# Attention over a dilated window and a long convolution: a new step order, with PSUM pool and copy engine chosen per step

## The chip, the cores and the metric

The kernel runs on one core of one Trainium2 chip. The metric is device time in microseconds (us) of one execution. The kernel before takes 263.62 us, the median of three runs (262.68 to 266.32).

The engines are TensorE (PE in the profile: matmuls and transposes; PEld: its weight loads), VectorE (DVE), ScalarE (ACT), GpSimd (POOL), and SyncE (SP), which only issues transfers here. Transfers between DRAM and SBUF, and within SBUF, are run by 16 DMA engines. Matmul results land in PSUM and have to be copied out by VectorE or ScalarE before TensorE may use the place again; this copy is called evacuation below.

## The reference

Two independent halves share the program, and their outputs are concatenated along the last axis.

```python
def _A_ref(x, wqkv, wo):                       # S=2048, D=576, 32 heads of 18
    W, dil = 8, 2
    qkv = (x @ wqkv) ...                       # q, k, v
    idx = pos[:, None] - off[None, :]          # 8 positions back, in steps of 2
    logits = einsum("bhsd,bhswd->bhsw", q, kg) * scale    # kg, vg: gathered k, v
    logits = where(idx >= 0, logits, -1e9)
    o = einsum("bhsw,bhswd->bhsd", softmax(logits), vg)
    return o.reshape(B, S, D) @ wo

def _B_ref(q, k, v, shift_k, ssm_k, ssm_D):
    k_shift = ...                              # 4-tap causal convolution of k along S
    kv = k_shift * v
    y = irfft(rfft(kv, 2S) * rfft(ssm_k, 2S))[:S]         # causal convolution, length S
    return q * (y + kv * ssm_D)

out = concatenate([a, b], axis=-1)
```

All tensors are bf16.

## The kernel before

The program is a list of some 300 steps. Each is a short Python function that emits a few instructions; the string `ORDER` says in which order they are emitted. A scheduler below it may still move an instruction a little, as far as data allows. The instruction stream of each engine is then fixed: an engine that waits for something lets nothing behind pass.

Half A: `xt` transposes x by TensorE, `qk` and `qt` project q and k (`qt` for the last 64 channels), `v` projects v, `lm` multiplies q by shifted k on VectorE, `lb` sums over a head's channels by TensorE, `sa`/`sb` are the softmax, `at` transposes the weights, `ha` copies v's edge rows to the neighbouring partition, `pm` multiplies weights by v, `ps` sums over the window by TensorE, `po` is the output projection. Half B: `sk` and `cv` are the short convolution, `ia` makes tables, `sx`/`kp` are the first stage of the transforms of kv and of the filter, whose results go to DRAM (`Dx`, `Dk`), `kl`/`xl` load them in another layout, `ks`/`xs` are the second stage, `gp` is the product of the spectra, `gi` the first stage back (to `Dy` in DRAM), `yl` loads that, `ys` is the last stage, with the multiplication by q. `kt` transposes the filter.

```python
pa = tile_pool(name="pa", bufs=2, space=PS)      # PSUM: two places in each of two pools,
pb = tile_pool(name="pb", bufs=2, space=PS)      # each [128, 2, 512] fp32
def psa(): return pa.tile([128, 2, 512], FP32, name="psA")
def psb(): return pb.tile([128, 2, 512], FP32, name="psB")
...
nc.scalar.dma_start(shr, B_shift_k ...)          # loads ahead of the steps, on SyncE's queue
load_x(0)
load_wq()                                        # q and k columns of wqkv, 1.3 MB
load_x(1)
load_kv(0)
load_x(2)
load_x(3)
...
def x_tr(qtr):                                   # one step: three groups of transposes
    for kp in range(3):
        ptr = pa.tile([128, 2, 1024], BF16, name="psA")
        ...                                      # 8, 8 and 4 transposes
        if kp == 1:
            nc.scalar.activation(dst, ptr[:, 0:n, 0:512], ACT.Copy)      # L288
        else:
            copy32(dst, ptr[:, 0:n, 0:512])      # L275, VectorE, as int32
...
nc.scalar.activation(wqt, wq.rearrange(...)[:, :, :, 128 * HC:D], ACT.Copy)   # L429
...
def qk_step(comp, cp, j):
    ps = psa()
    for u in range(2):
        for kb in range(5):
            nc.tensor.matmul(ps[:, u, :], wcols(kb, comp, 2 * cp + u), xT[:, kb, t], ...)   # L381
    nc.scalar.activation(..., ps[:], ACT.Copy)                                              # L382

def s1_part(src, key, c2, ch, Dd, add_d):        # sx and kp
    ps = psb()
    ...                                          # L417: 2 matmuls of 384 columns
    nc.scalar.activation(vst[:, :, 384 * ch:384 * ch + 384], ps[:, :, 0:384], ACT.Copy)     # L421
    if ch == 2:
        for dh, (d0, d1) in enumerate(DCH):
            nc.sync.dma_start(by_f1(Dd, dh, 4 * c2, 4), ...)     # to Dx or Dk; vst has two slots

def s2(Wt, g, dst, scale):                       # ks and xs: four groups each
    for prl in range(4):
        ps = psb()
        ...                                      # L549: 2 matmuls of 288 columns
        nc.scalar.activation(dst[:, 2 * prl:2 * prl + 2, :], ps[:, :, 0:HD], ACT.Copy, scale=scale)  # L551

def w_load(Dd, key, i):                          # kl, xl; Wr has three slots, shared with yl
    nc.sync.dma_start(Wr.get((key, i)), by_rt(Dd, i // 4, i % 4))

def k_spec(i):                                   # ks; Kr has two slots
    Kc = Kr.get(i)
    s2(Wr[("k", i)], i % 4, Kc[:, 0], 1.0 / 2048)
    nc.gpsimd.dma_start(Kc[0:64, 1], Kc[64:128, 0])      # the swap of the halves, within SBUF
    nc.gpsimd.dma_start(Kc[64:128, 1], Kc[0:64, 0])

def g_inv(i, hv):                                # gi; Yr has two slots
    for prl in (2 * hv, 2 * hv + 1):
        ps = psb()
        ...                                      # L582: 4 matmuls of 288 columns
        nc.scalar.activation(Y[:, 2 * prl:2 * prl + 2, :], ps[:, :, 0:HD], ACT.Copy)   # L584
    if hv:
        nc.sync.dma_start(by_rt(Dy, dh, g), Y)

def y_load(i):                                   # needs all four Dy stores of its half
    nc.sync.dma_start(Wr.get(("y", i)), by_f1(Dy, dh, 8 * c4, 8))
    nc.gpsimd.dma_start(qtr.get(i), qb[...])
# y_step (ys): L657, 4 matmuls; L658, the VectorE product that also empties PSUM
# p_sum (ps): L618; p_mul (pm): L604; p_out (po): L637, L639; l_mul (lm): L486; l_sum (lb): L496, L502
```

Of the kernel before, what the change touches and what calls it, by code (L numbers as in the profile page):

```python
# [9 lines left out]
ACT = mybir.ActivationFunctionType  # L10
# [8 lines left out]
xt.0 sk qk.0.0.0 qk.1.0.0 cv.0 qk.1.1.0 qk.0.1.0 lkv.1 xt.1 xt.2 qk.0.1.1 lkv.2 xt.3 ia qk.1.0.1 sx.0.0 lwv sx.0.1  # L19
qk.1.1.1 sx.0.2 sx.1.0 qk.1.0.3 sx.1.1 cv.1 sx.1.2 qk.0.0.1 sx.2.0 cv.2 sx.2.1 sx.2.2 qk.1.0.2 sx.3.0 lkn qt.0  # L20
qk.1.1.2 sx.3.1 qk.0.0.2 sx.3.2 sx.4.0 qk.0.1.2 sx.4.1 qk.0.0.3 sx.4.2 lkv.3 sx.5.0 qt.3 cv.3 sx.5.1 qk.0.1.3 qt.2
sx.5.2 qt.1 qk.1.1.3 sx.6.0 kt.0 v.1 sx.6.1 v.2 sx.6.2 v.0 sx.7.0 lm.0.0 sx.7.1 kt.1 sx.7.2 kp.0.0 lm.1.0 lm.0.1
lm.0.2 lb.0 lm.1.1 lm.1.2 kp.0.1 lm.2.0 lb.1 v.3 kp.0.2 kp.1.0 v.4 v.5 lm.3.0 ha.0 lm.2.1 kp.1.1 kt.2 kp.1.2 kp.2.0
lm.2.2 lb.2 kp.2.1 lm.3.1 lm.3.2 v.7 lb.3 kt.3 kp.2.2 v.6 lm.4.0 kt.4 kp.3.0 kp.3.1 kp.3.2 kp.4.0 sa.0 kp.4.1 kp.4.2
kt.5 kp.5.0 lm.4.1 sb.0 v.8 lm.4.2 lm.5.0 v.9 lb.4 lm.5.1 v.10 kt.6 kp.5.1 v.11 kp.5.2 lm.5.2 lb.5 kp.6.0 at.0 ha.1
v.13 kt.7 lm.6.0 v.15 lm.6.1 kp.6.1 v.14 ha.2 kp.6.2 kp.7.0 lm.6.2 lb.6 kp.7.1 v.12 lm.7.0 lm.7.1 lwo lm.7.2 ha.3
kp.7.2 kl.0 xl.0 lb.7 ks.0 xs.0 kl.1 xl.1 ks.1 sa.1 kl.2 pm.0.0 ps.0.0 gp.0.0 gi.0.0 pm.0.1 xl.2 xs.1 gp.0.1 pm.1.0
gp.1.0 ps.0.1 ks.2 xl.3 xs.3 gp.1.1 xs.2 gi.0.1 gp.2.0 gi.1.0 xl.4 ps.1.0 gp.2.1 gi.1.1 kl.3 kl.4 gi.2.0 pm.1.1 ks.3
pm.2.0 ps.1.1 po.0.0 xs.4 ks.4 po.0.1 gp.3.0 xl.5 gi.2.1 pm.2.1 kl.5 ps.2.0 gp.3.1 ks.5 po.1.0 sb.1 pm.3.0 ps.2.1
gi.3.0 po.1.1 gp.4.0 gp.4.1 at.1 gi.3.1 kl.6 ps.3.0 pm.3.1 xs.5 pm.4.0 po.2.0 gp.5.0 xl.6 gi.4.0 ps.3.1 gp.5.1 gi.4.1  # L30
yl.0 xs.6 ks.6 ys.0.0 xl.7 gi.5.0 po.2.1 ps.4.0 kl.7 ks.7 pm.4.1 po.3.0 xs.7 gp.6.0 ys.0.1 ps.4.1 gi.5.1 yl.1 gi.6.0
gp.6.1 gp.7.0 po.3.1 pm.5.0 yl.2 ys.1.0 po.4.0 pm.5.1 ys.1.1 gi.6.1 ys.2.0 pm.6.0 ps.5.0 gi.7.0 ps.5.1 gp.7.1 gi.7.1
yl.3 po.4.1 pm.6.1 ys.2.1 yl.4 ps.6.0 ys.3.0 ys.3.1 po.5.0 po.5.1 pm.7.0 yl.5 ps.6.1 ys.4.0 ys.4.1 po.6.0 ys.5.0 yl.6
ps.7.0 po.6.1 yl.7 ys.5.1 pm.7.1 ps.7.1 ys.6.0 ys.6.1 po.7.0 ys.7.0 ys.7.1 po.7.1
# [4 lines left out]
def kernel(  # L39
# [19 lines left out]
    HC = 4  # L59
# [16 lines left out]

    def psa():
        return pa.tile([128, 2, 512], FP32, name="psA")

    def psb():  # L80
        return pb.tile([128, 2, 512], FP32, name="psB")
# [146 lines left out]
    def load_wq():  # L228
        nc.sync.dma_start(wq[:, 0:4, :], A_wqkv[0:512, 0:2 * D].rearrange("(kb p) a -> p kb a", p=128))
        nc.sync.dma_start(wq[0:64, 4, :], A_wqkv[512:576, 0:2 * D])  # L230
# [25 lines left out]
    load_x(0)  # L256
    load_wq()
    load_x(1)
    load_kv(0)
    load_x(2)  # L260
    load_x(3)

# [11 lines left out]
    def copy32(dst, src):  # L274
        nc.vector.tensor_single_scalar(dst.bitcast(I32), src.bitcast(I32), 0, ALU.bitwise_or)  # L275

    def x_tr(qtr):
        for kp in range(3):
            n = 2 if kp < 2 else 1
            ptr = pa.tile([128, 2, 1024], BF16, name="psA")  # L280
            for u in range(n):
                kb = 2 * kp + u
                col0 = 128 * kb
                for lsb in range(4):
                    nc.tensor.transpose(ptr[:, u, 128 * lsb:128 * lsb + 128], xns[qtr][:, lsb, col0:col0 + 128], ident[:])
            dst = xT[:, 2 * kp:2 * kp + n, 512 * qtr:512 * qtr + 512]
            if kp == 1:
                nc.scalar.activation(dst, ptr[:, 0:n, 0:512], ACT.Copy)  # L288
            else:
                copy32(dst, ptr[:, 0:n, 0:512])  # L290
# [73 lines left out]
    def v_step(t2):  # L364
        ps = psa()
        for di, (d0, d1) in enumerate(DCH):
            for kb in range(5):
                nc.tensor.matmul(ps[:, di, 0:288], xTt[:, kb, t2, :], wv[:, kb, d0:d1], start=(kb == 0), stop=(kb == 4))  # L368
        nc.scalar.activation(vX[:, 14 + t2, :].rearrange("p (d i h) -> p d i h", i=2, h=16),
                             ps[:, :, 0:288].rearrange("p i (h d) -> p d i h", d=DH), ACT.Copy)  # L370
# [4 lines left out]
    def qk_step(comp, cp, j):  # L375
        pad = PADL if comp else 0
        ps = psa()
        t = slice(512 * j, 512 * j + 512)
        for u in range(2):
            for kb in range(5):  # L380
                nc.tensor.matmul(ps[:, u, :], wcols(kb, comp, 2 * cp + u), xT[:, kb, t], start=(kb == 0), stop=(kb == 4))  # L381
        nc.scalar.activation((k2 if comp else q2)[cp][:, :, pad + 512 * j:pad + 512 * j + 512], ps[:], ACT.Copy)  # L382

    def qk_tail_step(j):
        ps = psa()
        hh, t = j // 2, slice(512 * j, 512 * j + 512)
        for kb in range(5):
            nc.tensor.matmul(ps[:, 0, :], wqt[:, kb].rearrange("p c d -> p (c d)"), xT[:, kb, t], start=(kb == 0), stop=(kb == 4))
        r, o = slice(64 * hh, 64 * hh + 64), 512 * (j % 2)
        nc.scalar.activation(qh[r, o:o + 512], ps[0:64, 0, :], ACT.Copy)  # L390
        nc.scalar.activation(kh[r, PADL + o:PADL + o + 512], ps[64:128, 0, :], ACT.Copy)
        if j == 1:
            nc.scalar.activation(kh[64:128, 0:PADL], ps[64:128, 0, 512 - PADL:512], ACT.Copy)

    def ia_tables():
        for g in range(8):
            ps = psb()
            for v in range(4):
                for zi in range(2):
                    for hp in range(2):  # L400
                        nc.tensor.matmul(ps[64 * hp:64 * hp + 64, zi, 128 * v:128 * v + 128],
                                         W2[:, 4 * g + v, zi].rearrange("p l f -> p (l f)"),
                                         nident[:] if hp > zi else ident[:], start=True, stop=True, tile_position=(0, 64 * hp))
            nc.scalar.activation(IAt[:, :, 4 * g:4 * g + 4, :].rearrange("p z v t -> p z (v t)"), ps[:], ACT.Copy)
        ptr = pb.tile([128, 2, 1024], BF16, name="psB")
        for ri in range(2):
            nc.tensor.transpose(ptr[:, 0, 128 * ri:128 * ri + 128], T1[:, ri, :], ident[:])
        nc.vector.tensor_copy(IB[:], ptr[:, 0, 0:256].rearrange("p (a b) -> p a b", a=2))


    def s1_part(src, key, c2, ch, Dd, add_d):
# [9 lines left out]
        nc.scalar.activation(vst[:, :, 384 * ch:384 * ch + 384], ps[:, :, 0:384], ACT.Copy)  # L421
# [7 lines left out]
    nc.scalar.activation(wqt, wq.rearrange("p k (c d) -> p k c d", c=2)[:, :, :, 128 * HC:D], ACT.Copy)  # L429

    def sk_step():
        for i in range(3):
            n = 256 if i < 2 else 64
            ps = psb()
            for u in range(2 if i < 2 else 1):
# [3 lines left out]
            nc.scalar.activation(skb[:, :, 256 * i:256 * i + n],  # L439
                                 ps[:].rearrange("p u (d j) -> p j (u d)", j=4)[:, :, 0:n], ACT.Copy)  # L440
# [19 lines left out]
    def k_tr(c2):  # L460
        kt = ktr.get(c2)
        ptr = pb.tile([128, 2, 1024], BF16, name="psB")
# [28 lines left out]
    def l_sum(n):  # L491
# [13 lines left out]
        nc.scalar.activation(Lh[hf][:, 2 * wp:2 * wp + 2, :], psw[:, 0, :].rearrange("p (u t) -> p u t", u=2), ACT.Copy)  # L505
# [28 lines left out]
    def at_step(hf):  # L534
        L = Lh[hf].rearrange("p w (a b) -> p w b a", b=2)
        pst = pa.tile([128, 2, 4, 2, 128], BF16, name="psA")
# [4 lines left out]
        for u in range(2):  # L541
            nc.scalar.activation(ath[hf][:, 4 * u:4 * u + 4].rearrange("p w b j h -> p w b (j h)"), pst[:, u], ACT.Copy)  # L542


    def s2(Wt, g, dst, scale):
        for prl in range(4):
# [4 lines left out]
            nc.scalar.activation(dst[:, 2 * prl:2 * prl + 2, :], ps[:, :, 0:HD], ACT.Copy, scale=scale)  # L551
# [11 lines left out]
    def x_spec(i):  # L563
        s2(Wr[("x", i)], i % 4, Xr.get(i), 1.0)
        Wr.drop(("x", i))
# [8 lines left out]
    def g_inv(i, hv):  # L574
        dh, g = i // 4, i % 4
        Y = Yr[i] if hv else Yr.get(i)
        for prl in (2 * hv, 2 * hv + 1):
# [6 lines left out]
            nc.scalar.activation(Y[:, 2 * prl:2 * prl + 2, :], ps[:, :, 0:HD], ACT.Copy)  # L584
# [26 lines left out]
    def p_sum(tp, u):  # L611
        if u == 0:
            oTr.get(tp)
            oaccs[tp] = pa.tile([128, 2, 4, 128], FP32, name="psA")
# [8 lines left out]
        nc.scalar.activation(oTr[tp][:, 0:4].rearrange("p c u t -> p u c t"), oaccs[tp][:], ACT.Copy)  # L623
# [4 lines left out]
        nc.scalar.activation(oTr[tp][:, 4, 0, :], otl[:, 0, 0:128], ACT.Copy)  # L628
        tlr.drop(tp)

    def p_out(tp, u):
# [7 lines left out]
        nc.scalar.activation(stage[:, u, :].rearrange("p (i d) -> p i d", i=2), ps[:, :, 0:288], ACT.Copy)  # L639
# [25 lines left out]
    STEP = dict(xt=x_tr, ia=ia_tables, sk=sk_step, qk=qk_step, qt=qk_tail_step, lkv=load_kv, lwv=load_wv, lkn=load_knat,  # L665
# [3 lines left out]
    for item in ORDER.split():  # L669
        name, *args = item.split(".")  # L670
        STEP[name](*map(int, args))

# [29 lines left out]
```

## Time and profile before

| Engine | what most of its time is | busy, us | mean of one, ns |
|---|---|---|---|
| TensorE | L381, q and k projections, 160 matmuls | 40.7 | 403 |
| TensorE | L618, window sums, 512 matmuls | 40.2 | 227 |
| ScalarE | L551, evacuations of ks and xs, 64 | 38.0 | 652 |
| ScalarE | L421, evacuations of sx and kp, 48 | 37.4 | 811 |
| VectorE | L486, q times shifted k, 32 | 37.9 | 1225 |
| VectorE | L604, weights times v, 16 | 36.6 | 2289 |

The profiled execution spans 265.8 us, and its DMA queues move 55.24 MB, 208 GB/s on average. A page of the profile gives the busy time of each engine, then the span in 40 equal slices (one digit for each slice and engine: tenths busy; PEclk is the granted clock of TensorE in tenths), the chain of work that ended last, followed back from the end, and the costliest groups of instructions by line of the kernel. A busy TensorE isn't TensorE at its peak, since matmuls overlap; and idle time of an engine matters only where the chain runs through it.

### The profile page before, as it was taken

Reading aid. Unit: us, or ns where it says so; the run is one execution under the profiler, and the core shown is the slowest. Engines: PE = TensorE matmul, PEld = TensorE weight load, DVE = VectorE, ACT = ScalarE, POOL = GpSimd, SP = SyncE. Lnnn points to the kernel's source line nnn. Section 1 sums busy time; section 2 is a strip of 40 time slices with the busy share of each in tenths; the row PEclk is TensorE's granted clock in tenths of the full one; section 3 lists DMA queues with packets and bytes.
Section 4 is the critical chain, followed back from the end, with each engine's and each line's share of the span. In section 5 each row is a group of like instructions: output and inputs, shape, how many; then the busy total and the mean of one; then the engine's idle time right before and its main releaser. Section 6 shows DMA issues by size and latency. Waiting matters only on the chain.

```text
span 265.8 us, 4987 instructions
## 1 busy us (share of the span) xinstructions
PE 228.5 (86%) x2013; PEld 153.0 (58%) x2013; DVE 190.5 (72%) x211; ACT 173.2 (65%) x252; POOL 25.2 (9%) x62
## 2 busy tenths in 40 slices
PE   2689899999999999996946799796999881999893
PEld 2225665444573747565614676575987660698782
DVE  1667989999968878989647798847496484277232
ACT  0566978978984657968466699694789761162321
POOL 8700000000000000002010110030200210101100
PEclk9999999999999999999995999998999998599999
DMA  7999943823433435737799869389678899157994
GB/s 239 307 333 370 304 109 113 249 71 111 126 91 120 132 92 149 209 86 202 240 231 316 274 166 306 154 252 302 168 260 270 239 230 313 35 165 228 325 293 133
DMA packets 43759, 55.24 MB, mean 208 GB/s; under 512 B 2285, under 2 KB 36285, under 8 KB 43737
## 3 DMA queue, kind: packets, MB, share of 16 engines
q1 hardware_dynamic: 41766, 47.71, 59.4%
q0 software_dynamic: 1968, 7.23, 10.1%
q8 instruction: 15, 0.25, 0.4%
q14 instruction: 8, 0.06, 0.1%
q10 hardware_dynamic: 2, 0.00, 0.0%
HBM read 29.27 MB, written 18.87 MB: 181 GB/s over the span
## 4 chain that ended last, share of the span: by engine, by line
PE 57%; DMA 24%; ACT 12%; issue 2%; SPq 2%; DVE 1%; POOL 0%; ACTq 0%; DVEq 0%; POOLq 0%
PE psA L381 13%; DMA area<-area 7%; DMA area<-Dy 7%; PE psA L368 7%; PE psA L618 7%; PE psB L417 5%; PE psA L502 5%; PE psA L637 5%; PE psB L549 4%; PE psB L657 3%; DMA area<-in_A_wqkv_dram 3%; PE psB L582 3%; ACT area L421 2%; DMA area<-Dk 2%; DMA Dy<-area 2%
## 5 line engine op out<-in xcount | busy, mean ns | idle before, releaser
L604 DVE TENSOR_TENSOR area<-area,area 128x4096 bf16<-128x4096 bf16 x16 | 36.6, 2289 | 7.7 <-PE psA L618 3.2
L551 ACT ACTIVATE area<-psB 128x576 bf16<-128x576 f32 x64 | 38.0, 652 | 6.2 <-PE psB L549 3.3
L421 ACT ACTIVATE area<-psB 128x768 bf16<-128x768 f32 x48 | 37.4, 811 | 7.1 <-PE psB L417 6.7
L381 PE MATMUL psA<-area,area 128*128 128x512 bf16 x160 | 40.7, 403 | 1.3 <-ACT area L288 1.3
L486 DVE TENSOR_TENSOR area<-area 128x2048 bf16<-128x2048 bf16 x32 | 37.9, 1225 | 4.7 <-PE psA L502 4.7
L618 PE MATMUL psA<-ident,area 128*128 128x128 bf16 x512 | 40.2, 227 | 0.2 <-ACT area L623 0.2
L618 PEld LDWEIGHTS <-area 128*128 128x128 bf16 x512 | 35.2, 102 | 4.4 <-DVE area L604 0.6
L549 PE MATMUL psB<-area,W 128*128 128x288 bf16 x128 | 27.0, 301 | 10.8 <-DMA area<-Dx 4.8
L568 DVE TENSOR_TENSOR area<-area,area 128x2304 bf16<-128x2304 bf16 x16 | 21.2, 1355 | 16.2 <-DMA area<-area 15.0
L381 PEld LDWEIGHTS <-area 128*128 128x128 bf16 x160 | 16.0, 102 | 22.5 <-issue 7.5
L658 DVE TENSOR_TENSOR area<-psB,area 128x576 bf16<-128x576 f32 x16 | 11.7, 754 | 20.3 <-PE psB L657 18.6
L584 ACT ACTIVATE area<-psB 128x576 bf16<-128x576 f32 x32 | 19.9, 656 | 9.8 <-PE psB L582 7.0
L637 PE MATMUL psA<-wv,area 128*128 128x288 bf16 x160 | 26.2, 296 | 0.1
L639 ACT ACTIVATE area<-psA 128x576 bf16<-128x576 f32 x16 | 10.4, 652 | 23.8 <-PE psA L637 19.6
L417 PE MATMUL psB<-area,T 128*128 128x384 bf16 x96 | 22.2, 327 | 1.8 <-ACT area L421 1.6
L368 PE MATMUL psA<-wv,area 128*128 128x288 bf16 x160 | 23.0, 288 | 0.7 <-ACT area L542 0.7
L446 DVE TENSOR_TENSOR area<-area,area 128x2304 bf16<-128x2304 bf16 x16 | 21.5, 1353 | 2.4 <-ACT area L439 2.2
L368 PEld LDWEIGHTS <-area 128*128 128x128 bf16 x160 | 20.0, 145 | 5.0 <-issue 4.1
L382 ACT ACTIVATE area<-psA 128x1024 bf16<-128x1024 f32 x16 | 16.4, 1023 | 9.8 <-PE psA L381 9.7
L549 PEld LDWEIGHTS <-W 128*128 128x128 bf16 x128 | 12.2, 101 | 18.0 <-issue 8.0
L582 PE MATMUL psB<-area,IAt 128*128 128x288 bf16 x128 | 19.9, 290 | 3.1 <-DVE area L568 1.8
L648 POOL DMA_DIRECT2D area<-in_B_q_dram x8 | 6.1, 766 | 147.0 <-PE psA L540 116.0
(116 smaller groups left out, 295.6 us busy)
## 6 DMA issues: line engine op xcount, KB each, us to landing
Dx<-area SPq DMA_DIRECT2D x16, 288.0 KB, 3.1
Dk<-area SPq DMA_DIRECT2D x16, 288.0 KB, 3.4
area<-Dk SPq DMA_DIRECT2D x8, 576.0 KB, 6.3
area<-Dx SPq DMA_DIRECT2D x8, 576.0 KB, 5.2
area<-area POOLq DMA_DIRECT2D x16, 288.0 KB, 6.6
Dy<-area SPq DMA_DIRECT2D x8, 576.0 KB, 5.0
out_dram<-area SPq DMA_DIRECT2D x16, 288.0 KB, 3.7
area<-Dy SPq DMA_DIRECT2D x8, 576.0 KB, 7.9
```

Of the source, the lines that this page charges most:

```text
L368: nc.tensor.matmul(ps[:, di, 0:288], xTt[:, kb, t2, :], wv[:, kb, d0:d1], start=(kb == 0), stop=(kb == 4))
L381: nc.tensor.matmul(ps[:, u, :], wcols(kb, comp, 2 * cp + u), xT[:, kb, t], start=(kb == 0), stop=(kb == 4))
L417: nc.tensor.matmul(ps[:, ri, 0:384], T1[:, ri, :], sf[:, 384 * ch:384 * ch + 384], start=True, stop=not extra)
L421: nc.scalar.activation(vst[:, :, 384 * ch:384 * ch + 384], ps[:, :, 0:384], ACT.Copy)
L446: nc.vector.tensor_tensor(dst, kfull[:, 4 * c + 3 - j:4 * c + 7 - j, :], skb[:, j, :].unsqueeze(1).to_broadcast([128, 4, D]), ALU.mult)
L486: nc.vector.tensor_tensor(dst[:, u], halves(q2[h], hf), halves(k2[h][:, :, shs[u]:shs[u] + S], hf), ALU.mult)
L549: nc.tensor.matmul(ps[:, hp, 0:HD], W2[:, 8 * g + 2 * prl + hp].rearrange("p i l f -> p (i l f)"), Wt[:, 2 * prl + hp, :], start=True, sto ...
L551: nc.scalar.activation(dst[:, 2 * prl:2 * prl + 2, :], ps[:, :, 0:HD], ACT.Copy, scale=scale)
L582: nc.tensor.matmul(ps[:, hp, 0:HD], IAt[:, zi, 8 * g + hl, :], Pp[(i, hv)][:, zi, hl % 4, :], start=(zi == 0), stop=(zi == 1))
L604: nc.vector.tensor_tensor(P.rearrange("p w (d h) -> p w d h", h=H), vs[:, :, 0:16], at.to_broadcast([128, W, 16, H]), ALU.mult)
L618: nc.tensor.matmul(oaccs[tp][:, u, ct, :], P[:, wi, 128 * ct:128 * ct + 128], ident[:], start=(ct == 0 and wi == 0), stop=(wi == W - 1 and ...
L637: nc.tensor.matmul(ps[:, di, 0:288], lhs, wot[:, ct if ct < 4 else 4 + u, d0:d1], start=(ct == 0), stop=(ct == 4))
```

## The change

It leaves every operation of the computation as it is and touches three things. The first is the order of the steps, with the loads of x, of wq (now in two halves, q's columns and k's) and of the short filter's inputs placed among them, and the copy `wqt` as a step of its own. The second is a suffix on a step: `a` or `b` names the PSUM pool, `v` or `s` the engine that evacuates (VectorE or ScalarE); without a suffix it stays at the default. The third is that a transposition of x becomes three steps, one for each pair of channel blocks, which may go apart. Order, pools and engines come from a model of the engines' queues. The aim is that TensorE waits less for free PSUM places, for copies behind others in one queue, and for transfers.

```diff
 ORDER = """
-xt.0 sk qk.0.0.0 qk.1.0.0 cv.0 qk.1.1.0 qk.0.1.0 lkv.1 xt.1 xt.2 ... ia qk.1.0.1 sx.0.0 lwv ...
... (the rest of the old order stands in the whole kernel)
+lx.0 lwq.0 lx.2 xt.0.0:bs lx.1 sk:b lwq.1 xt.0.1:sa lkv.0 lkv.1 xt.0.2:v qk.0.1.0:bs cv.0 qk.0.0.0:sa lx.3 qk.1.0.0
+xt.1.0:bs xt.1.2:v lkv.2 xt.1.1:s qk.1.1.0:sa xt.2.0:a ia xt.2.2:s wt:s xt.3.2:va xt.3.0:b xt.3.1:sa sx.0.0:av cv.1
+sx.0.1:a sx.0.2:s qk.0.1.1 sx.1.0:b qk.0.0.1:a sx.1.1:sb sx.1.2:s lwv qk.1.0.1 cv.2 qk.1.0.3:sb xt.2.1:sa sx.2.0:sb
... (cut)
+v.9:s v.10:s lm.5.0 v.11:a kp.5.0 kp.5.1:bs lm.5.1 lm.5.2 kp.5.2 kp.6.0:a at.0:s lb.5:bs kt.7:bv lm.6.0 v.13:va
+kp.6.1:sb kp.6.2:s v.14:s lm.6.1 kp.7.0:bs v.15:s kp.7.1:bs lm.6.2 lb.6:s lm.7.0 v.12:a lm.7.1 kp.7.2:b lwo ha.2 ha.3
+lm.7.2 lb.7:av kl.0 xl.0 ks.0:b kl.1 xl.1 xs.0 ks.1:a kl.2 pm.0.0 xs.1:b pm.0.1 xl.2 gp.0.0 gi.0.0 gp.0.1 ks.2:sb
+xs.2:vb gp.1.0 xl.3 sa.1 xl.4 pm.1.0 gi.0.1:s gp.1.1 gp.2.0 ps.0.0:as ps.0.1:s ps.1.0:s xs.3 kl.3 ks.3:sb gi.1.0:bs
+kl.4 pm.1.1 gi.1.1:b ps.1.1:as gp.2.1 gp.3.0 pm.2.0 gi.2.0:av ks.4:s sb.1 xl.5 xs.4:s gi.2.1 po.0.0 kl.5 po.0.1:sb
+ps.2.0:v gp.3.1 gp.4.0 pm.2.1 ks.5:b ps.2.1:b po.1.0:bs pm.3.0 xs.5:a po.1.1:as gi.3.0:sb gi.3.1:bs kl.6 at.1 gp.4.1
+pm.3.1 ps.3.0:a ps.3.1:a gi.4.0:sa pm.4.0 gi.4.1:sa gp.5.0 xl.6 ks.6:as xs.6:b yl.0 gp.5.1 pm.4.1 po.2.0:sb gp.6.0
+gi.5.0:v ys.0.0 pm.5.0 po.2.1:sa xl.7 kl.7 ks.7:v ps.4.0:as yl.1 pm.5.1 xs.7:sb po.3.0:v ps.4.1:sa ys.0.1:b po.3.1:sb
+yl.2 yl.3 gi.5.1:a ps.5.0:a pm.6.0 gp.6.1 gp.7.0 ys.1.0 ys.1.1 gi.6.0:bs gi.6.1:a ys.2.0:b ps.5.1:b gi.7.0:a ys.2.1
+gp.7.1 pm.6.1 po.4.0:sb gi.7.1:s yl.4 yl.5 ys.3.0:b po.4.1:v po.5.0:b ys.3.1:b ps.6.0:bv ps.6.1:av po.5.1:bs pm.7.0
+pm.7.1 po.6.0:s yl.6 ys.4.0:a ps.7.0:s ys.4.1 ys.5.0:a yl.7 po.6.1:av ys.5.1 ps.7.1:s ys.6.0:b po.7.0:a po.7.1:s
+ys.6.1:b ys.7.0:b ys.7.1:a
 """
+    how = {"ps": None, "ev": None}
+
+    def psum(default, *shape, dt=FP32):
+        a = (how["ps"] or default) == "a"
+        return (pa if a else pb).tile([128, *shape], dt, name="psA" if a else "psB")
...
+    def evac(dst, src, scale=None, on="s"):
+        if (how["ev"] or on) == "s":
+            nc.scalar.activation(dst, src, ACT.Copy, **({} if scale is None else {"scale": scale}))
+        elif scale is None:
+            nc.vector.tensor_copy(dst, src)
+        else:
+            nc.vector.tensor_scalar(dst, src, scale, None, op0=ALU.mult)
...
-    def load_wq():
-        nc.sync.dma_start(wq[:, 0:4, :], A_wqkv[0:512, 0:2 * D].rearrange("(kb p) a -> p kb a", p=128))
-        nc.sync.dma_start(wq[0:64, 4, :], A_wqkv[512:576, 0:2 * D])
+    def load_wq(c):
+        d = slice(D * c, D * c + D)
+        nc.sync.dma_start(wq[:, 0:4, d], A_wqkv[0:512, d].rearrange("(kb p) a -> p kb a", p=128))
+        nc.sync.dma_start(wq[0:64, 4, d], A_wqkv[512:576, d])
...
-    load_x(0)
-    load_wq()
-    load_x(1)
-    load_kv(0)
-    load_x(2)
-    load_x(3)
...
-    def x_tr(qtr):
-        for kp in range(3):
+    def x_tr(qtr, kp):
+        if True:
...
-            if kp == 1:
-                nc.scalar.activation(dst, ptr[:, 0:n, 0:512], ACT.Copy)
-            else:
-                copy32(dst, ptr[:, 0:n, 0:512])
+            copy32(dst, ptr[:, 0:n, 0:512])
...
-        nc.scalar.activation((k2 if comp else q2)[cp][:, :, pad + 512 * j:pad + 512 * j + 512], ps[:], ACT.Copy)
+        evac((k2 if comp else q2)[cp][:, :, pad + 512 * j:pad + 512 * j + 512], ps[:])
... (the other evacuations of matmul results likewise become evac)
-    nc.scalar.activation(wqt, wq.rearrange("p k (c d) -> p k c d", c=2)[:, :, :, 128 * HC:D], ACT.Copy)
+
+    def wqt_step():
+        evac(wqt, wq.rearrange("p k (c d) -> p k c d", c=2)[:, :, :, 128 * HC:D])
...
     for item in ORDER.split():
+        item, _, mods = item.partition(":")
         name, *args = item.split(".")
+        how["ps"] = next((m for m in mods if m in "ab"), None)
+        how["ev"] = next((m for m in mods if m in "vs"), None)
         STEP[name](*map(int, args))
```

## The prediction

> **What bounds the kernel now.** I read the page's busy shares first, then the slices, then who TensorE waits for, then the chain of waits with its times, and at last a table of stretches.
>
> The page, engines and slices:
>
> ```profile
> PE 228.5 (86%) x2013; PEld 153.0 (58%) x2013; DVE 190.5 (72%) x211; ACT 173.2 (65%) x252; POOL 25.2 (9%) x62
> PE   2689899999999999996946799796999881999893
> PEclk9999999999999999999995999998999998599999
> DMA  7999943823433435737799869389678899157994
> ```
>
> TensorE (PE) is the fullest engine, and nearly solid from 40 to 120 us (slices 7 to 18; a slice is 6.6 us). Its holes are at the start and after 130 us, and there the DMA row is full. The two slices with clock 5 follow two of those holes.
>
> What TensorE waits for, in us, times, longest:
>
> ```profile
> PE psB L657 <- DMA area<-Dy: 6.9, 2, 5.9
> PE psA L285 <- DMA area<-in_A_x_dram: 5.2, 1, 5.2
> PE psB L549 <- DMA area<-Dx: 4.8, 1, 4.8
> PE psB L549 <- ACT area L551: 2.7, 2, 2.0
> PE psB L549 <- ACT area L584: 2.1, 2, 1.9
> ```
>
> The long waits are for transfers; those for a copy out of PSUM (L551 and L584 are ScalarE evacuations) are short.
>
> The chain of waits (start, length, what):
>
> ```profile
> 1.84 7.65 DMA area<-in_A_wqkv_dram
> 9.59 1.28 ACT L429
> 10.88 0.74 ACT area L429
> 11.62 0.91 ACT area L288
> ...
> 15.68 9.44 PE psA L381 x34
> ...
> 163.55 5.66 DMA Dy<-area
> ...
> 174.05 6.54 DMA area<-area
> ...
> 214.31 11.65 DMA area<-Dy
> ```
>
> Two things are to be seen. ScalarE stands behind L429, the copy of the weights' tails, until the whole of wq is there; only then does it evacuate the first transposes (L288). And the late part of the chain alternates between transfers of 6 to 12 us and short work.
>
> Stretches (PE, PEld, DVE, ACT, POOL busy, clock, DMA share, GB/s):
>
> ```profile
> 134.50:149.40 14.90, 7.71 (x61) 5.06 (x58) 9.11 (x10) 9.65 (x14) 2.10 (x4) 0.77 1.02 286
> 173.80:187.40 13.60, 11.57 (x113) 9.56 (x111) 6.77 (x6) 9.03 (x17) 2.65 (x5) 0.87 0.96 288
> 208.40:231.00 22.60, 15.35 (x119) 10.92 (x120) 11.63 (x11) 10.14 (x17) 1.82 (x3) 0.86 0.79 213
> ```
>
> In the first two the transfers are saturated at 286 to 288 GB/s, and no engine is full.
>
> To place the loss I gave each matmul its full-rate time (ten of 512 columns take 2.16 us in the chain, 0.216 each; others by their columns, four side by side in L496/L502 as two), added these in program order, and took the sum from the time at which a step really begins. The sum is 197.6 us. "Lost" so far: 13.1 us when xt.1 begins (24.9 us), 15.9 at 40 us, 16.9 at 77, 21.3 at 103, 27.7 at ks.0 (134.5), 33.7 at xs.0 (141.5), 37.8 at gi.0.0 (149.4), 41.1 at gi.2.0 (166), 43.5 at ps.2 (173.8), 48.5 at gi.3.0 (187.4), 53.4 before ys.1.0, 59.7 when it begins (226.0), 62.4 at gi.7.1, 64.0 at the end; then 4 us of tail. So 36 of 64 us are lost after 134 us, and only some 4 between 25 and 77 us.
>
> **What the Trainium skill says.** "TensorE: Matmul & The Clock Gate", section "What's actually happening": an idle window of about 3.4 us halves the clock and about 3.4 us of work restores it. The trace agrees: after the 5.9 us hole before 226.0, ten matmuls of L637 take 2.40 us instead of 1.22. A long hole thus costs about 2 us more. "VectorE: DVE Perf Modes", "Why PSUM operands drop a tier": fp32 from PSUM is at 1x. The trace's nearest row agrees: L658, 576 fp32 columns from PSUM, 754 ns, against 652 ns for ScalarE's L551. The same copy is thus no cheaper on VectorE (DVE); it only moves. "DMA: Bandwidth & Descriptors", "Issuing engines are not separate DMA queues": all queues share the same 16 engines. The stretches agree: the SyncE loads and the GpSimd swaps are slow together.
>
> **The change part by part.**
>
> *Copies moved.* By the new program's instruction order 25 evacuations go from ScalarE to VectorE: 12 of 576 columns in ks/xs/gi, 3 in po, 1 in v, 5 of 768 in sx/kp, 1 qk, 1 ps and its tail, 1 lb. ScalarE loses 15 x 0.654 + 5 x 0.811 + 0.654 + 2 x 1.02 + 0.60 + 0.27 = 17.4 us and gains 3 more transposes (2.7) and one kt (about 1.1): 173.2 - 13.6 = 159.6 us. VectorE gains, at 0.754 for 576 and about 0.95, 1.22 and 0.28 for 768, 1024 and 128 (0.754 changed by 1 ns a column, an estimate from that row and L275), 20.2 us, less 2.5 for transposes: about 208 us. Neither becomes the fullest engine. In 40 to 60 us VectorE is already at 19.6 of 20 us; summing its list in order (convolutions 32 x 1.35, the W2 products 2.4, copies 6.3, first products 3.7) it finishes the last convolution near 72 us, and sx.6.0 wants it near 74. Enough, barely.
>
> *Start.* wq comes in halves, q first, and the wqt copy has left the head of ScalarE's queue. 1.24 MB (x0 and half of wq) then gate the first projection instead of 1.9 MB. By ScalarE's new order (table load from 6.2, transposes at 7.5 and 10.3 us, the sine between) the first projection is through at about 15.0 us, where before 6 of its 10 matmuls were done at 15.6. Until 40 us the new order packs the eight L404 table copies (1.04 us each on ScalarE, 0.57 on PE) close together: PE stands about 2.5 us for them. Lost at 40 us: about 14.7 instead of 15.9. Gain **1.2 us**.
>
> *Middle, to ks.0.* The last third has the same steps in nearly the same order (from kp.5.2 on all positions agree within 2.1 us of work), so most of the 10.8 us lost from 77 to 134 us stays. kp.7.1 now follows at.0 and v.13, so that it doesn't stand for the Dk store and ScalarE (0.8 us lost at 120 to 122). Gain **0.8 us**. The hole of 4.8 us before xs.0 stays: its load still stands in SyncE's queue behind lwo and the halos, which wait for v.12, with lb.7 and ks.0 alone between.
>
> *ks.0 to ys.1.0.* Positions in the summed work: ks.2 2.6 us earlier, xs.2 4.7, ks.3 4.6, ks.4 3.9, xs.5 5.8, gi.0.1 3.5 earlier; gi.1.0 1.4 later. What this buys: the store of Y 0 goes out earlier and gi.2.0 comes 0.5 later, so that ScalarE's wait for Dy (2.1 us at 169, the two-slot Y ring) goes; the swap of ks.3 starts 4.6 us earlier, so that gp.3 doesn't stand for it (in the 4.0 us lost from 173.8 to 187.4). If both were free: 6 us. But the transfers limit it: from 134.5 us to gi.3.0 the old kernel moved about 14.0 MB in 52.9 us (from the GB/s row of the slices, about 265 on average); the new one needs one load more by then (x 5), 14.6 MB, which is 50.7 us at 288 GB/s. So at most **2.2 us** here, and about 2 is what I take. From gi.3.0 to ys.1.0, 9.8 MB took 38.6 us, now 9.2 MB, 32 us at best. Y load 1 gets its slot from ks.7, with 7.9 us of work up to ys.1.0 instead of 7.3; the transfer took 15.4 us (210.6 to 226.0). So this hole stays, shortened by 0.6 us plus part of the 6 us of room. I take **2 us**.
>
> *End.* From gi.7.1's end to ys.4.0 there are 9.6 us of work instead of 9.1: gain 0.5. The program now ends with three multiplications on VectorE (0.75 each) instead of one ScalarE copy (0.65): loss 0.5. Together 0.
>
> Sum: 1.2 + 0.8 + 2 + 2 = 6.0 us. I take 0.9 off for waits that a new order makes and I don't see: 263.6 - 5.1 = **258.5 us**.
>
> **Rivals.**
> 1. *Transfers rule the second half.* For it: 1.02, 0.96 and 0.79 shares in the three stretches. Against it: slices 22 to 28 have shares of 6, 9, 3, 8, 9, 6, so there is room in between. Then only start and middle count: about 262 us.
> 2. *The evacuations were the bound, and the better balance frees the second half.* For it: ScalarE is busy 17.3 of 20 us from 160 to 180, and VectorE waits 15.0 us there for the swaps. Against it: TensorE's waits for L551 and L584 sum to 4.8 us. The holes shorten, with their slow clock after them: 6 plus 6 plus 4 us, about 250.
> 3. *VectorE becomes the bound.* It has 17.6 us more and in-order waits for PSUM between convolutions that had no slack. For it: 19.6 of 20 us in 40 to 60. Against it: the list above ends before its reader. A late convolution pushes everything behind it: 266 to 269.
>
> **Range and chances.** Start and middle are worth 0 to 4 us, the second half 0 to 10, an unseen wait -5 to 0: **251.5 to 266**. 2% below 263.6 is 258.3, just under my centre: faster 0.46, same 0.46, slower 0.08.
>
> **What would show it.** Right: ScalarE's first activation before 8 us, and qk solid from about 15 us; L98 rows on VectorE of about 0.75 us for 576; VectorE near 208 us and ScalarE near 160; the ACT wait on Dy gone; gi.3.0 about 4 us earlier; still a hole of 4 to 5 us before xs.0 and one before ys.1.0, each with a slow clock behind it. Wrong: a hole of TensorE between 40 and 75 us for a convolution or copy on VectorE (rival 3); the DMA share near 1 all the way from 134 to 215 us with the same end (rival 1); or the hole before ys.1.0 gone (rival 2).

## The result, and the profile after

| | median, us | lowest to highest | executions |
|---|---|---|---|
| before | 263.15 | 261.06 to 266.32 | 4 |
| after | 252.87 | 252.44 to 254.59 | 4 |

The ratio is 0.965, with a 95% interval of 0.957 to 0.973. The change gains about 10 us; the prediction had 5. Executions more than 1.5% above the fastest of their kernel are left out of every ratio and interval below, so that a ratio can lie nearer to 1 than that of the medians.

After, the page's engines and slices (a slice is now 6.3 us):

```profile
PE 222.8 (89%) x2007; PEld 150.5 (60%) x2013; DVE 206.9 (82%) x232; ACT 161.0 (64%) x231; POOL 25.4 (10%) x62
PE   1999899999999999999872599799999998999991
PEclk9999999999999999999996589999999999999998
DMA  6999994420336173918799779889978899968974
```

VectorE has 16 us more and ScalarE 12 us less, as worked out. One of the two slow-clock places is gone, that near the end. The other, slices 22 to 24, is still there, and longer. What TensorE waits for, after (us, times, longest; L563 is ks and xs, L671 is ys, L300 the transposes of x):

```profile
PE psB L563 <- DMA area<-Dx: 6.9, 2, 4.8
PE psB L300 <- DMA area<-in_A_x_dram: 5.2, 1, 5.2
PE psB L563 <- DMA area<-Dk: 1.4, 1, 1.4
PE psB L671 <- DMA area<-Dy: 1.0, 1, 1.0
PE psB L413 <- ACT IAt L96: 1.0, 3, 0.3
```

The longest line of before, 6.9 us for Dy, is 1.0 here. The wait for Dx has not shrunk. The waits for a ScalarE copy (L96 is now the line of all of ScalarE's evacuations) are of 0.2 to 0.8 us each.

The chain of waits after (start, length, what):

```profile
0.81 4.31 DMA area<-in_A_x_dram
5.17 1.04 PE psB L300 x8
...
9.30 3.10 PE psA L393 x7
12.72 1.24 PE psA L393 x3
13.96 2.16 PE psB L393 x10
...
152.52 7.12 DMA area<-area
...
202.95 8.75 DMA area<-area
```

At the start the load of the weights and L429 have left the chain: from 5.17 us on it is TensorE's own work, and the first projection ends at 13.96. Late in the chain the transfers of Dy have gone; the swaps within SBUF are still there. The three stretches that correspond to those of before (PE, PEld, DVE, ACT, POOL busy, clock, DMA share, GB/s):

```profile
129.50:144.00 14.50, 6.15 (x28) 3.07 (x27) 9.80 (x11) 8.47 (x12) 1.08 (x2) 0.63 0.96 271
165.00:180.60 15.60, 15.13 (x154) 11.95 (x152) 14.82 (x16) 12.87 (x24) 2.36 (x5) 1.00 0.97 285
196.00:211.00 15.00, 13.72 (x145) 10.91 (x144) 13.57 (x14) 7.76 (x14) 2.34 (x5) 1.00 0.95 244
```

The first is as poor as before. In the other two TensorE is nearly full, while the transfers run at the rate of before (285 against 288 GB/s) and above it (244 against 213).

With the prediction's measure (the start of a step, less the full-rate matmul work ahead of it), from one profile each; the three middle columns are experiments told below:

| lost by, us | before | L429 moved | Y load moved | three edits | after |
|---|---|---|---|---|---|
| xt.1 | 13.1 | 9.9 | 12.8 | 9.0 | 8.4 |
| sx.2.0 | 16.0 | 13.0 | 15.7 | 12.1 | 12.6 |
| ks.0 | 27.7 | 24.6 | 27.3 | 23.8 | 22.6 |
| xs.0 | 33.7 | 30.8 | 33.3 | 30.2 | 28.6 |
| gi.3.0 | 48.5 | 42.8 | 46.1 | 40.9 | 41.2 |
| ys.0.1 | 52.0 | 46.5 | 49.8 | 45.7 | 44.1 |
| ys.1.0 | 59.7 | 52.8 | 51.1 | 47.7 | 45.3 |
| last matmul | 64.2 | 56.7 | 54.4 | 50.5 | 48.4 |
| from there to the end | 4.0 | 4.0 | 4.1 | 4.0 | 5.1 |

From before to after: 3.4 us up to sx.2.0, 1.7 more up to ks.0, nothing at xs.0, about 2 up to gi.3.0, 0.6 up to ys.0.1, then 6.5 between ys.0.1 and ys.1.0. From ys.1.0 to the last matmul it is 1.4 more, and 1.1 goes back after that. The places are read from this, not the sizes: the profiled execution of before is one of its longer ones, and the spans differ by 14.7 us where the medians differ by 10.3.

### The profile page after: what moved, and what is told of

The parts are those of the page before. It is cut to its first block, busy times and chain, and to the rows that moved or that the text cites. A ratio compares the mean times of both kernels' runs of the same rounds, so it can differ in the third digit from the quotient of the medians.

```text
span 251.1 us, 4991 instructions
## 1 busy us (share of the span) xinstructions
PE 222.8 (89%) x2007; PEld 150.5 (60%) x2013; DVE 206.9 (82%) x232; ACT 161.0 (64%) x231; POOL 25.4 (10%) x62
## 3 DMA queue, kind: packets, MB, share of 16 engines
q0 software_dynamic: 1968, 7.23, 10.7%
## 4 chain that ended last, share of the span: by engine, by line
PE 59%; DMA 10%; issue 10%; ACT 8%; DVE 7%; SPq 2%; POOL 1%; DVEq 0%; ACTq 0%; POOLq 0%
PE psA L393 10%; ACT area L96 8%; PE psA L380 7%; DMA area<-area 6%; PE psA L516 5%; PE psA L632 5%; PE psB L393 4%; PE psA L651 4%; PE psB L429 4%; PE psB L651 3%; DMA Dk<-area 2%; DVE area L618 2%; DMA area<-in_A_x_dram 2%; PE psB L596 2%; PE psB L632 1%
## 5 line engine op out<-in xcount | busy, mean ns | idle before, releaser
L96 ACT ACTIVATE area<-psB 128x576 bf16<-128x576 f32 (+6 forms) x124 | 84.6, 714 | 42.3 <-PE psB L563 13.4
L96 ACT ACTIVATE area<-psA 128x576 bf16<-128x576 f32 (+6 forms) x91 | 66.1, 753 | 38.7 <-PE psA L632 12.3
L618 DVE TENSOR_TENSOR area<-area,area 128x4096 bf16<-128x4096 bf16 x16 | 36.6, 2285 | 6.2 <-DMA area<-area 2.0
L632 PEld LDWEIGHTS <-area 128*128 128x128 bf16 x512 | 32.6, 99 | 2.6 <-issue 0.5
L632 PE MATMUL psA<-ident,area 128*128 128x128 bf16 x448 | 32.0, 222 | 0.2 <-ACT area L96 0.2
L563 PE MATMUL psB<-area,W 128*128 128x288 bf16 x104 | 21.5, 306 | 9.4 <-DMA area<-Dx 6.9
L393 PEld LDWEIGHTS <-area 128*128 128x128 bf16 x160 | 15.8, 100 | 19.6 <-issue 3.2
L393 PE MATMUL psA<-area,area 128*128 128x512 bf16 x105 | 27.1, 401 | 0.2
L582 DVE TENSOR_TENSOR area<-area,area 128x2304 bf16<-128x2304 bf16 x16 | 21.2, 1350 | 6.5 <-DMA area<-area 6.5
L380 PEld LDWEIGHTS <-area 128*128 128x128 bf16 x160 | 19.7, 145 | 6.3 <-issue 5.7
L563 PEld LDWEIGHTS <-W 128*128 128x128 bf16 x128 | 12.6, 105 | 17.9 <-DMA area<-Dx 7.9
L380 PE MATMUL psA<-wv,area 128*128 128x288 bf16 x160 | 22.2, 288 | 0.9 <-ACT area L96 0.8
L651 PEld LDWEIGHTS <-area 128*128 128x128 bf16 x160 | 15.4, 97 | 5.8 <-issue 1.0
L429 PE MATMUL psB<-area,T 128*128 128x384 bf16 x74 | 17.2, 326 | 1.0 <-DVE area L290 0.4
L465 DVE TENSOR_TENSOR area<-area 128x2304 bf16<-128x2304 bf16 x12 | 16.2, 1352 | 0.2
L516 PE MATMUL psA<-area,Eh 128*32 128x512 bf16 x112 | 15.7, 632 | 0.0
L596 PEld LDWEIGHTS <-IAt 128*128 128x128 bf16 x128 | 12.2, 97 | 5.6 <-issue 2.5
L651 PE MATMUL psA<-wv,area 128*128 128x288 bf16 x90 | 13.3, 286 | 1.0 <-DVE area L98 0.7
```

The source lines that it names most:

```text
L96: nc.scalar.activation(dst, src, ACT.Copy, **({} if scale is None else {"scale": scale}))
L429: nc.tensor.matmul(ps[:, ri, 0:384], T1[:, ri, :], sf[:, 384 * ch:384 * ch + 384], start=True, stop=not extra)
L516: nc.tensor.matmul(psw[32 * j:32 * j + 32, 0, :].rearrange("p (u a b) -> p u a b", u=2, b=2), Eh[:, 2 * h + c, :], prr[(n, h)][:, :, c, :, ...
L563: nc.tensor.matmul(ps[:, hp, 0:HD], W2[:, 8 * g + 2 * prl + hp].rearrange("p i l f -> p (i l f)"), Wt[:, 2 * prl + hp, :], start=True, sto ...
L582: nc.vector.tensor_tensor(Pp.get((i, hv)), Kr[i][:, :, 4 * hv:4 * hv + 4, :], Xr[i][:, 4 * hv:4 * hv + 4, :].unsqueeze(1).to_broadcast([12 ...
L618: nc.vector.tensor_tensor(P.rearrange("p w (d h) -> p w d h", h=H), vs[:, :, 0:16], at.to_broadcast([128, W, 16, H]), ALU.mult)
```

## The experiments

The theory after reading the two traces: two single waits carry the gain. One is ScalarE's block at the start. The other is the load of Y 1, which takes another slot of the three-slot ring and so is issued earlier. Rival: it is the balance, the 25 copies given to VectorE and the pools, that lets TensorE run on.

**Y load 1 early, in the kernel before (label b_yl1).**

```diff
-... ks.7 pm.4.1 po.3.0 xs.7 gp.6.0 ys.0.1 ps.4.1 gi.5.1 yl.1 gi.6.0
+... ks.7 yl.1 pm.4.1 po.3.0 xs.7 gp.6.0 ys.0.1 ps.4.1 gi.5.1 gi.6.0
```

> The kernel before with one step moved: yl.1 right behind ks.7, so that it takes the slot that ks.7 leaves and no longer the one that ys.0.1 leaves. Theory (the slot of that one load made the hole before ys.1.0): the load goes out near 210.6 us instead of 214.3, the hole of 5.9 us and the slow clock behind it go nearly whole, 255 to 258 us. Rival (the hole closed because the copies are balanced or the transfers come earlier everywhere): 262 to 263 us.

Measured: 259.65 us (257.23 to 262.28), before beside it 263.56 (258.88 to 267.73 in 40 executions); ratio 0.992 (0.988 to 0.997). The gain is 3.9 us by the medians and 2.1 (0.9 to 3.2) by the ratio: more than the rival had, less than the theory. The instruction order of all engines but the load queue is that of before. SyncE's queue (issue start, length, what), before:

```profile
210.63 4.54 SPq L647 DMA_DIRECT2D area<-Dy  x3
```

These are three Y loads, issued at 210.63, 213.4 and 214.31 us; Y load 1 is the *third*, since yl.1 stands behind ys.0.1 in the order and gets the slot that ys.0.1 sets free. The two ahead of it (Y 2 and 3, not needed for long) have the bandwidth first. With yl.1 behind ks.7 it takes ks.7's slot and is the first of the three, issued at 208.39:

```profile
208.39 4.50 SPq L647 DMA_DIRECT2D area<-Dy  x3
```

Its wait and the same stretch as in the prediction, in this experiment:

```profile
PE psB L657 <- DMA area<-Dy: 1.1, 1, 1.1
```

```profile
208.40:231.00 22.60, 20.81 (x235) 17.29 (x234) 16.89 (x16) 13.88 (x24) 2.58 (x4) 1.00 0.88 248
```

TensorE is busy for 20.81 us instead of 15.35, at clock 1.00 instead of 0.86. One moved word takes the hole and the slow clock behind it away. The table has the stretch from ys.0.1 to ys.1.0 for four profiles of the old order: 7.7 and 6.3 us are lost in it with the late slot, 1.3 and 2.0 with the early one.

**The reverse, in the kernel after (a_yl1back).** yl.1 moved from behind ps.4.0 to behind ys.0.1.

> The changed kernel with yl.1 moved back behind ys.0.1, whose slot it then has to take. Theory: the hole before ys.1.0 is back with 5 to 7 us, 257 to 261 us. Rival: 253 to 254 us.

Measured: 256.08 us (253.97 to 258.57), ratio 0.984 (0.971 to 0.997) to the kernel before beside it. That is 3.2 above the median of after, which was not run beside it, and between theory and rival. In its profile the wait for Dy is 1.9 us instead of 1.0: the scheduler put the window sums of ps.5 ahead of ys.1.0 as filler. In this profile the late slot costs less, since other work is at hand. The size is not settled by this run: its profiled execution is the fastest of the four.

**The 25 copies back on ScalarE (a_nov).** The kernel after with its order and pools; the evacuations moved to VectorE go back.

> The changed kernel with the 25 evacuations of matmul results given back to ScalarE, order and PSUM pools as changed. Theory (the order of steps and slots made the gain): 253 to 256 us. Rival (the balance of copies made it): 258 us or more.

Measured: 255.61 us (255.21 to 257.99), ratio 0.987 (0.976 to 0.998). This is 2.7 above the median of after, which was not run beside it. The engines:

```profile
PE 224.2 (88%) x2013; PEld 151.7 (60%) x2013; DVE 190.0 (75%) x207; ACT 175.5 (69%) x256; POOL 25.4 (10%) x62
```

ScalarE is again fuller than in the kernel before (173.2). The time lies where the theory had it: 8.0 us below the kernel before beside it by the medians, but only 3.4 (0.5 to 6.4) by the ratio, so that this run alone doesn't say what share the balance has. The run with three edits, below, does: it has none of the copies on VectorE. In the new order they are worth some 2.7 us by the medians; in the profiles 1.4 of it appears between sx.2.0 and ks.0, 2 after ys.1.0.

**L429 off ScalarE (b_wqtpool).** The copy of the weights' tails alone goes to another engine.

```diff
-    nc.scalar.activation(wqt, wq.rearrange(...)[:, :, :, 128 * HC:D], ACT.Copy)
+    nc.gpsimd.tensor_copy(wqt, wq.rearrange(...)[:, :, :, 128 * HC:D])
```

> The kernel before with the copy of the weights' tails (L429) on GpSimd instead of ScalarE; the queues of SyncE and VectorE are unchanged. Theory: of the 4.7 us that the changed kernel gains by xt.1 and the 3.4 us that are left of it at 40 us, most comes from ScalarE not standing at the head of its queue for all of wq. Then the time lost when xt.1 begins falls from 13.1 to about 11 us, at 40 us from 15.9 to about 14, and the total from 263.2 to about 261 us. Rival: the order of the loads (half of wq, then x) is the cause; then xt.1 still begins with 12.6 us or more lost and the total stays within 1 us of 263.

Measured: 261.2 us (258.98 to 263.2) against 264.1; ratio 0.987 (0.980 to 0.994), so about 3 us. xt.1 begins with 9.9 us lost instead of 13.1, more than expected. ScalarE's timeline before (start, length; in brackets the idle time ahead and what ended it):

```profile
9.59 1.28 ACT L429 ACT_TABLE_LOAD   x1 [9.59 <-DMA area<-in_A_wqkv_dram]
10.88 0.74 ACT L429 ACTIVATE area<-area 128x640 bf16<-128x640 bf16 x1
11.52 1.00 ACT L288 ACTIVATE area<-psA 128x1024 bf16<-128x1024 bf16 x1
```

and in this experiment:

```profile
1.35 1.28 ACT L288 ACT_TABLE_LOAD   x1 [1.35 <-PEq L686]
7.02 1.02 ACT L288 ACTIVATE area<-psA 128x1024 bf16<-128x1024 bf16 x1 [4.38 <-PE psA L285]
```

With L429 at its head, ScalarE did nothing until the whole of wq had landed; even the table load that comes ahead of the first activation stood behind that wait. Without it the table is loaded at 1.35 us, in time that costs nothing, and the evacuation of x's transposes runs at 7.02 instead of 11.52. The order of the loads, the rival, is unchanged here: wq is still one load. The scheduler did interleave some of TensorE's steps after xt.1 otherwise; but the gain is there when xt.1 begins, and ahead of that a single matmul of sk changed its place.

**Three edits together (b_yl1start).** The kernel before with Y load 1 early, L429 on GpSimd, and the memset of L223 (1.53 us at the head of GpSimd's queue, ahead of the ones that sk waits for) moved to just before it.

> The kernel before with three small edits: Y load 1 emitted right behind ks.7, L429 on GpSimd, and the memset of the k tile's head moved from the front of GpSimd's queue to just before it. Theory: start and Y load are independent and add up: 3.9 us from the Y load as measured, about 3 from the start, 256 to 257.5 us. Rival: what is won at the start is waited for again at the transfers between 134 and 190 us; then it is no better than the Y load alone, 259 to 260 us.

Measured: 254.34 us (253.30 to 255.38) against 264.1; ratio 0.964 (0.959 to 0.969). That is the ratio of the whole change. It is also less time than the theory had: the parts make 3.9 and 2.9 us by their medians, and 0.9 for the memset in the profile, 7.7 together, where 9.8 are measured. The other 2 us are not explained; they may lie between ks.0 and gi.3.0, where none of the three edits is and where the profile loses 3.7 us less than that of before. The slices:

```profile
PE   2999899999999999997881999979999977999793
PEclk9999999999999999999996599999999999999998
```

The PE row has the one deep hole that after has too, in slice 22. The kernel after, run once more on another chip (**after2**), took 253.21 us (252.59 to 254.50), ratio 0.961 (0.955 to 0.967).

> The changed kernel once more, on the same chip as the three below, so that they can be set against it: 252 to 254.5 us, with the same waits (Dx 6.9 us in two, Dk 1.4, Dy 1.0) to within 0.5 us each.

The waits were 6.4 us for Dx and 1.7 for Dk, those of the first profile of after to within 0.5; the wait for Dy, 1.0 there, is missing here. By the medians after2 is 10.0 us faster than the kernel before beside it, the three edits 9.8, and the two intervals overlap. So it isn't shown that the new order, pools and copy engines together are worth anything beyond the three edits; set against each other directly, on two chips, the medians differ by 1 to 1.5 us. The memset's part is seen in sk, which starts at 7.37 instead of 8.41 us.

**Without the pools (a_nopool).** The suffixes `a` and `b` taken out of the order.

> The changed kernel without its choice of PSUM pools (a and b suffixes removed; order and copy engines stay). Theory: the pools are worth little, since TensorE's waits for a copy out of PSUM sum to only some 5 us in the kernel before; 252 to 255 us. Rival: the order was made for these pools, and without them the evacuations stand in the way of transposes and sx; 257 us or more, with waits of TensorE for ScalarE or VectorE of over 4 us more by 60 us.

Measured: 271.85 us (271.08 to 274.21), 19 us above after and 8 above before: my theory was wrong by far. Its longest waits, and VectorE's timeline:

```profile
PE psA L632 <- DVE area L618: 10.7, 1, 10.7
PE psB L563 <- DMA area<-Dk: 8.3, 4, 3.7
```

```profile
146.88 2.63 DVE L582 TENSOR_TENSOR area<-area,area 128x2304 bf16<-128x2304 bf16 x2 [9.26 <-DMA area<-area]
149.42 2.28 DVE L618 TENSOR_TENSOR area<-area,area 128x4096 bf16<-128x4096 bf16 x1
```

The scheduler, given other pools, put the product gp.0 (L582, which needs the swap of ks.0) ahead of pm.0 (L618), and X load 0 elsewhere. VectorE stood 9.3 us for a transfer with ready work behind it, and ps.0 (L632) waited for that work. Of 18 us lost more than in after, 4.3 were there by ks.0 and 5.7 more between ks.0 and xs.1. This run therefore doesn't measure the pools alone: they also change what the scheduler does with the same list.

**The hole before xs.0: X load 0 first (a_xl0), wo later (a_lwo).** In a_xl0, K load 0, X load 0 and K load 1 stand ahead of wo and the halos in the order; in a_lwo only wo moves, behind kl.3.

> The changed kernel with xl.0 and kl.1 moved ahead of lwo and the halos, which stand in front of them in the SyncE queue. Theory (the hole of 4.8 us before xs.0 is a queue order): xl.0 goes out near 125 us instead of 131.4, the hole shrinks to under 2 us, 248 to 250 us. Rival (the transfers are the limit there): the wait moves to the next load or to the halos, 252 to 254 us.

> The changed kernel with the load of wo moved behind kl.3, so that X load 0 doesn't stand behind it and the halos in SyncE's queue. Theory: the hole of 6 us before xs.0 shrinks by 3 us or more, and since wo (needed first by po.0.0) then shares the transfers later, half of that stays; 250 to 252 us. Rival: the transfers are saturated from 128 us on, and VectorE takes gp.0 ahead of pm.0 as it did when X load 0 was put first; xs.1 begins at the same time and ps.0 later, 254 to 258 us.

Measured: 258.71 us (256.56 to 262.60) and 254.78 (253.17 to 255.39). The ratios to the kernel before beside each are 0.989 (0.984 to 0.993) and 0.965 (0.960 to 0.970); after has 0.965. So a_xl0 is slower than after, and worse than even its rival had it; a_lwo, in its rival's range, gained nothing, and a loss isn't shown (its median is 1.9 above that of after). The hole before xs.0 went in both (23.5 and 24.6 us lost when xs.0 begins instead of 28.6). But in a_xl0 xs.1 began at 143.25 us, no earlier than in after (142.65):

```profile
PE psB L563 <- DMA area<-Dx: 7.6, 2, 7.0
PE psA L632 <- DVE area L618: 3.7, 1, 3.7
```

```profile
129.00:148.00 19.00, 5.60 (x32) 2.80 (x28) 8.28 (x10) 10.00 (x15) 2.10 (x4) 0.67 1.00 255
```

The transfers are full for 19 us on end; a load that goes earlier pushes the next one later. And VectorE's order turns as in the run without pools. In a_lwo xs.1 did begin earlier, at 138.54 us, against its rival; but ps.0 began later, at 147.11 instead of 145.03, as the rival had it. VectorE's order is what took the gain back; the longest wait and VectorE's timeline:

```profile
PE psA L632 <- DVE area L618: 7.0, 1, 7.0
```

```profile
142.22 2.63 DVE L582 TENSOR_TENSOR area<-area,area 128x2304 bf16<-128x2304 bf16 x2 [8.25 <-DMA area<-area]
```

**v.12 earlier, X load 0 in another slot (a_v12, a_v12b), and the tail (a_tail).** Meant to beat after. v.12 goes ahead of lb.6, the halos and X load 0 follow it, and the ring's first slot is the one under xT; a_v12b moves wo behind X load 1 as well. All three end with a new tail:

```diff
-ps.7.1:s ys.6.0:b po.7.0:a po.7.1:s ys.6.1:b ys.7.0:b ys.7.1:a
+ps.7.1:s ys.6.0:b ys.6.1:b po.7.0:a ys.7.0:b ys.7.1:b po.7.1:s
```

> The changed kernel with v.12 ahead of lb.6, the halos and X load 0 right behind it, X load 0 in the slot that lies under xT (free as soon as v.12 has read it) instead of one under the filter's buffers, and the last steps as in the run on the tail. wo stays between the halos and K load 0. Theory: halos, wo and X load 0 move into a stretch in which the transfers have room (119 to 125 us), the hole of 6 us before xs.0 falls to 3 or less, and VectorE still takes pm.0 before gp.0; with 1 us of the tail 248 to 250.5 us. Rival: K load 0 and the swap of ks.0 then wait behind wo, and gp.0 begins no earlier than 142.9 us; 251.5 us or more.

> The same as the run with v.12 ahead of lb.6, but with the load of wo behind X load 1, so that it doesn't stand before K load 0. Theory: the hole goes nearly whole (2 us or less lost between ks.0 and xs.0), and wo is still there in time for po.0.0 near 165 us; 247 to 250 us. Rival: wo then shares the saturated transfers from 130 to 150 us with the loads and swaps, gp.0 comes later, and it is slower than its sister by 1 us or more.

> The changed kernel with its last steps in an order that ends with po.7.1 on ScalarE instead of three products on VectorE, and the last products in the PSUM pool that the output projection doesn't use. Theory: the 5.1 us from the last matmul to the end fall to about 4.0, as in the kernel before; 1 us faster than the changed kernel beside it. Rival: the end is set by the last stores, of which there are now as many; no difference, within 0.3 us.

Measured, beside after2 (253.21): a_v12 254.54 us (253.33 to 254.91), a_v12b 253.78 (253.42 to 255.89), a_tail 253.09 (251.07 to 254.29). VectorE did take pm.0 first in both, and the hole moved from xs.0 to ks.0, which now waits for its own load:

```profile
PE psB L563 <- DMA area<-Dk: 10.4, 4, 6.4
```

```profile
PE psB L563 <- DMA area<-Dk: 4.0, 1, 4.0
```

(a_v12, then a_v12b.) The rival held for a_v12, and neither held its theory's time. In a_v12 K load 0 is issued at 128.94 us instead of 124.86, behind the halos, X load 0 and wo. gi.0.0 begins at 147.6 and 147.9 us, in after at 147.3, in a_lwo at 150.0: none of these orders brings it forward. The tail falls from 5.1 to 4.3 us in the profile, but the medians don't differ, so that 0.8 us isn't shown. No version beat the kernel after measurably.

## Why the prediction was right in direction and small in size

The time fell inside the range, near its low end; but the range was wide (251.5 to 266), and "faster" and "same" had equal chances. Of the named signs, ScalarE's first activation (6.24 us), the end of its wait for Dy (2.1 us before) and an earlier gi.3.0 (180.6 instead of 187.4) came; and so did a sign of being wrong, the hole before ys.1.0 gone. Three readings were slips: VectorE's 15.0 us of waits for the swaps are those of the whole run, of which the longest (4.9) ends at 180.7; the DMA shares 6, 9, 3, 8, 9, 6 are of slices 24 to 29; and from 173.8 to 187.4 us its own list has 5.0 lost, not 4.0. By the prediction's own steps:

**Copies moved: right.** Predicted 208 and 159.6 us for VectorE and ScalarE, measured 206.9 and 161.0; no hole of TensorE for VectorE between 40 and 75 us (rival 3). The step said that this is no gain by itself. In the new order it is worth about 2.7 us by the medians (a_nov); on the old order it was not tried.

**Start: the term was too small, 1.2 against 3.4 us.** Mechanism right: ScalarE freed from L429. The size failed at "table load from 6.2, transposes at 7.5 and 10.3 us". I let the table load wait for the first transposes, and ScalarE's part of them with it. It ran at 1.36 us, the evacuations at 6.24 and 8.99, and the first projection ended at 13.96 instead of 15.0. L429 alone is worth 3.0 us at sx.2.0 (b_wqtpool), the memset 0.9 more; that one the prediction did not have. The reverse, L429 put back into the new order, was not run.

**Middle: 0.8 against about 1.7 us.** From sx.2.0 to ks.0 the table has 11.7 us lost before, 11.7 with three edits and 10.0 after. With the copies back on ScalarE it is 11.4 (23.5 less 12.1 in the profile of a_nov). The stretch takes 86.6 to 86.7 us in six profiles of the new order (after, after2, a_yl1back, a_xl0, a_lwo, a_tail) and 88.0 in that of a_nov. So it is the copies, and not kp.7.1's place, that give this gain.

**Hole before xs.0 stays: right**, 6.0 us lost between ks.0 and xs.0 in both kernels; the clock in the stretch is 0.77 before and 0.63 after. But its cause as the prediction had it, the load's place in SyncE's queue, was not the whole: a_xl0 and a_lwo took the load out of that place, the hole went, and TensorE waited later, before xs.1 in a_xl0 and for VectorE before ps.0 in both.

**ks.0 to gi.3.0: predicted 2, nothing shown.** The profiles give 20.8 us lost before and 18.6 after. But the stretch varies: with the same order as before in it, the experiments gave 18.2, 18.8 and 17.1. Whether the transfers bound the stretch as a whole, as the prediction had it, no run tests.

**gi.3.0 to ys.1.0: this step failed.** "Y load 1 gets its slot from ks.7, with 7.9 us of work up to ys.1.0 instead of 7.3; the transfer took 15.4 us (210.6 to 226.0). So this hole stays, shortened by 0.6 us plus part of the 6 us of room." The prediction took 2 us for the gain of this step; the profiles have 7.1 (11.2 us lost before, 4.1 after). In the old kernel Y load 1 didn't get its slot from ks.7, but from ys.0.1. It was the third of the loads issued from 210.63, at 214.31. The number stood in the prediction's own chain, "214.31 11.65 DMA area<-Dy", and I took the start of the group for the start of this load: the transfer took 11.65 us, not 15.4. In the new order it is the first, from 201.31:

```profile
201.31 6.55 SPq L661 DMA_DIRECT2D area<-Dy  x3
```

TensorE waits 1.0 us for it, and the clock isn't lost. Between ys.0.1 and ys.1.0 the gain is 6.5 us in the profiles; by itself, in b_yl1, it is 3.9 by the medians and 2.1 by the ratio. Rival 2 had the right sign for a wrong reason: the hole went because of a slot, not of the copies.

**End: 0 against -1.** The last matmul is followed by 5.1 us instead of 4.0: three VectorE products and their stores. The 0.5 us that were to be gained between gi.7.1 and ys.4.0 did not show apart.

## What to carry to other kernels

Follow each long wait for a load back to the instruction that frees its buffer: in a ring of slots, the place of the load in the program decides *whose* slot it takes, and one moved word was worth 2 to 4 us here. Ask of each queue what stands at its head at the start: one copy that waits for a large load cost 3.0 us on an engine with other work ready. And before a large reordering is credited with its gain, try the two or three waits it removed on the old order; here three small edits gave a ratio of 0.964, and the whole change 0.965.

## What I had not expected of the hardware

- The load of ScalarE's function table, 1.28 us, waits with the first activation when that one waits for a transfer (9.59 us), and ran without any wait at 1.35 where the first activation waits for TensorE. A first activation on a late load thus delays two things.
- In-order VectorE beside saturated transfers is sensitive: two products (2.63 us) put ahead of a ready one made it stand 8.3 to 10.3 us in three runs, and TensorE 3.7 to 10.7 us behind it.
- The same stretch with the same instructions, ks.0 to gi.3.0, lost 17.1 to 20.8 us in four profiles. A difference of 2 us there between two single profiles is no finding.
